# The order of the opening loads in a planned kernel: small parameters in front of the modulation weights and x rows

## The chip, the cores and the metric

The kernel runs on one core of one Trainium2 chip. The metric is the device time of one execution in microseconds; the time given is the median of three runs. Shorter is better.

## The reference

An x of 2048 tokens by 448 channels passes through two halves, each with an adaptive layer norm in front of it: a long convolution per channel, whose kernel is generated from state-space parameters, and a gated GELU block. Six modulation rows are computed from a small vector c.

```
x = A_u
mod = (_silu(c) @ w_mod).reshape(c.shape[0], 6, 1, -1)
sa, ca, ga, sb, cb, gb = (mod[:, 0], mod[:, 1], mod[:, 2], mod[:, 3], mod[:, 4], mod[:, 5])
h = _layernorm(x, axis=-1) * (1 + ca) + sa
x = x + ga * _A_ref(h, A_A_re, A_A_im, A_B_re, A_B_im, A_C_re, A_C_im, A_log_dt, A_Dskip)
h = _layernorm(x, axis=-1) * (1 + cb) + sb
x = x + gb * _B_ref(h, B_w_gate, B_w_up, B_w_down)
```

`_A_ref` makes, with dt = exp(log_dt), the convolution kernel K[d, l] as the real part of the sum over 256 states n of C dt B exp(dt A l), convolves it with h by an FFT of 4096 points, and adds h times Dskip. `_B_ref` is (gelu(h w_gate) * (h w_up)) w_down with an inner width of 1792.

## The kernel before, in words

The work is a list of 2018 small tasks, each a handful of instructions or DMAs on one engine. The function `s4_geglu` (line 413) makes them with `add` (line 473); each carries a name, an engine and its dependencies. Their order is written out by hand: the table `PLACE` (lines 40 to 263) gives every task a place, the n-th entry of a name for the n-th task of that name, and a letter behind the place picks the engine where there is a choice (a ACT, d DVE, p POOL, s SP). `Plan.order` (line 296) sorts by place and `Plan.run` (line 304) issues the tasks so. An engine works through its tasks in that order and waits at each for what it needs; tile buffers are also taken in that order.

The stages: an opening that loads parameters and rows; then, side by side, the generation of the convolution kernel (lines 629 to 755, 56 steps of exponentials, sines, products and small matmuls), the normalisation and first Fourier stage of x (lines 874 to 1006), and the transforms (lines 1068 to 1255); from about half of the span on the gated block (lines 1378 to 1680), bound by matmuls.

The tasks of the opening that matter here:

- p.ld.0 and p.ld.1 (`ld1`, lines 509 to 517, DMA at 512) load 448 and 224 KB of the state-space parameters for the first 112 channels, on ACT's queue. p.A1 (543) and p.A2 (548, 549) on DVE read the first; p.S1 (552, 553), p.S2 (570), p.S3 (571) on ACT, p.B1 (557 to 560), p.D1 (574 to 576) and p.B3 (579) on DVE follow; p.B2 (578) on ACT reads c.ld as well. dt (495, 496) on ACT reads c.ld, the log_dt vector. p.A3 (562) and p.C1 (565, 566) read p.ld.1 and dt. p.c0, d0, e0, f0 (481, 537, 539) split a result in three bfloat16 parts, which p.put0 (596) writes to DRAM from ACT's queue; lt0 (621) reads it back. p.put1 and lt1 do that with the second result.
- c.c (line 790) loads the vector c; silu (793) on ACT, which stands behind p.A3 in ACT's order, and sil2 (796 to 798) on DVE turn it into silu(c).
- m.ld.0, m.ld.1, m.ld.2 (`ldw`, line 806) load 784 KB of modulation weights each. m.mq0 (812) is the matmul of the third, m.cp0 (483) copies its partial sums, m.sm0 (823) adds them up; m.mm (816) makes the other two rows, with sixteen matmul instructions; m.ev (831, 834) evacuates, gs (860) multiplies two rows.
- x.ld.0 and x.ld.1 (853) load 896 KB of x each; bn (878, 879) takes their statistics, rstd (887) the roots, as (912) and norm (905) use them, ua (922) is the first Fourier matmul.
- c.ea (384 KB), c.rd (256 KB), c.au (64 KB), c.ak (128 KB; all through line 487) are constant tables; c.c and c.ld are 1.8 KB each. au is first read by as (912), ea and rd by the matmuls of lines 639 and 658, ak by line 771 much later.
- pad.0 (515) on POOL's queue copies 224 KB from DRAM to DRAM; d0 (865) and sel (842, 844) are memsets on POOL.
- p.ld.2 and p.ld.3 load 448 and 224 KB of parameters for the second 112 channels, from SP.

SP and ACT each own a queue for DMAs, and issue them in the order of their tasks. [...]

Of the kernel before, what the change touches and what calls it, by code (L numbers as in the profile page):

```python
# [40 lines left out]
    "anc": "121 137 143 162 152 204 207 247 264 309 333 340 348 356 445 456 469 485 502 517",  # L41
    "ang": "106 110 127 145 146 164 206 215 246 298 318 332 347 355 420 447 455 478 501 508 509 593 603 608 656 674 694 708 "
        "741 764 769 775 787 788 806 882 889 907 908 925 926 946 1005 1017 1018 1026 1039 1053 1114 1126 1135 1147 1153 1171 "
        "1184 1202",
    "as": "67d 75a 93d 109d 114d 130d 150a 176a 249d 254d 261a 283d 293d 329d 330d 352d",
    "bn": "45 46 59 57 39 47 48 55 230 236 232 234 184 228 196 201",
    "c.ai": "1266",
    "c.ak": "43",
    "c.au": "21",
    "c.c": "7",  # L50
    "c.ea": "20",
    "c.ih": "1280",
    "c.ld": "8",
    "c.rd": "25",
    "c.t1": "240",
    "co.adde": "1338 1339 1368 1340",
    "co.addl": "1383 1386 1419 1414",
    "co.addx": "1500 1510 1501 1520 1676 1714 1737 1684 1800 1812 1815 1806",
    "co.c2": "1586d 1593d 1587d 1590a 1758d 1760d 1772a 1770a 1893a 1907a 1906a 1900a",
    "co.ca": "1406a 1407a 1449a 1439a",  # L60
    "co.cb": "1415d 1413a 1452a 1441a",
    "co.h0": "1399a 1402a 1445d 1431a",
    "co.h2": "1534a 1576a 1568a 1557a 1750a 1746d 1761a 1766d 1855d 1888a 1842a 1874a",
    "co.l0": "1405 1411 1446 1432",
    "co.l2": "1538 1580 1570 1575 1752 1754 1762 1767 1856 1898 1851 1884",
    "co.mme": "1321 1335 1334 1337",
    "co.mml": "1378 1384 1408 1404",
    "co.mmx": "1488 1507 1489 1508 1653 1707 1735 1655 1791 1808 1810 1792",
    "co.n": "1390 1397 1444 1424",
    "co.nx": "1524 1573 1548 1532 1747 1745 1751 1763 1828 1876 1832 1872",  # L70
    "co.rc": "1389 1396 1427 1423",
    "co.rcx": "1522 1743 1825",
    "co.rt": "1387 1394 1421 1416",
    "co.rtx": "1521 1740 1816",
    "co.t2": "1560 1592 1571 1589 1755 1756 1765 1769 1882 1902 1868 1894",
    "co.ta": "1401 1403 1447 1437",
    "co.tb": "1409 1412 1448 1438",
    "cos": "523 609 624 635 686 687 713 711 756 773 798 797 805 820 819 887 902 910 924 940 950 957 1012 1028 1041 1044 1051 "
        "1066 1123 1133 1152 1167 1186 1195 1210 1225",
    "cos2": "126 141 144 163 158 205 213 256 276 317 334 342 354 359 446 463 482 488 506 530",  # L80
    "d.hi": "1564 1547 1584 1492 1528 1599 1502",
    "d.ld": "1562 1540 1582 1491 1514 1588 1497",
    "d.lo": "1569 1549 1585 1504 1533 1600 1513",
    "d0": "13",
    "dn": "1602 1605 1607 1608",
    "dn.k0": "1741 1889 1991",
    "dn.k2": "1753 1896 1998",
    "dn.k3": "1759 1899 2001",
    "dn.r": "1603 1606 1615 1631",
    "dn.r1": "1744 1962 2004",  # L90
    "dn.r4": "1768 1903 2002",
    "dn.r5": "1773 1908 2009",
    "dn.r6": "1775 1905",
    "dn.rh": "2003 2014 2016",
    "dn.s0": "2015",
    "dn.s1": "2017",
    "dn.st": "1650 1651 1621 1646 1774 1797 1786 1790 2008 2006 1979 1949 2011 2007 2010",
    "dn0": "1734 1738 1883 1886 1989 1990",
    "dn1": "1739 1891 1996",
    "dn2": "1764 1901 2005",  # L100
    "dn3": "1771 1904",
    "dn3h": "2012 2013",
    "dn4": "1749 1895 1999",
    "dn5": "1748 1892 1997",
    "dn6": "1757 1897 2000",
    "dsk": "195",
    "dt": "22",
    "e.f": "1664 1715 1702 1616 1645 1625 1683",
    "e.hi": "1666 1717 1703 1617 1652 1629 1687",
    "e.ld": "1649 1705 1700 1611 1644 1620 1679",  # L110
    "e.lo": "1667 1719 1704 1618 1658 1636 1689",
    "ev.end": "1252",
    "ev.fp": "705",
    "ev.geg": "1461",
    "ev.pq": "1332",
    "ev.ps": "1459",
    "ev.ub": "379",
    "ev.w0": "1369",
    "f.fc": "707 738 751 789 795 831 851 896 897 932 952 1019 1032 1060 1069 1105 1124 1142 1162 1180",
    "f.fwd": "740 757 780 809 834 850 877 898 917 945 964 995 1016 1033 1055 1076 1094 1118 1145 1154 1206 1214",  # L120
    "f.inv": "747 771 790 814 846 862 888 911 941 960 985 1013 1021 1050 1063 1089 1106 1129 1149 1173 1217 1232",
    "f.pr": "743 759 785 810 835 854 883 903 935 959 970 999 1020 1040 1062 1078 1104 1120 1148 1161 1207 1218",
    "f.st": "762 793 830 841 912 894 931 934 976 1008 1009 1030 1059 1090 1093 1112 1131 1157 1176 1190 1242 1241",
    "f.ut": "706 739 760 791 796 832 865 893 913 933 953 973 1006 1027 1035 1061 1079 1110 1130 1143 1174 1179",
    "f.z": "755a 774d 804a 822a 868a 866d 895d 922a 958d 982a 1000d 1014a 1038d 1052a 1084a 1098a 1125d 1140a 1164a 1188a "
        "1229a 1238a",
    "gs": "71 112",
    "gu": "1487 1498 1516 1517 1525 1542 1558 1559 1567 1578 1594 1614 1633 1634 1654 1656 1668 1671 1681 1685 1706 1710 "
        "1720 1721 1776 1777 1781 1793 1796 1809 1813 1823 1838 1839 1848 1853 1867 1869 1909 1912 1913 1922 1929 1931 1938 "
        "1939 1957 1958 1968 1969 1978 1980",  # L130
    "gu.g": "1429 1442 1450 1458 1463 1467 1474 1479 1496 1503 1518 1526 1543 1550 1563 1572 1583 1595 1609 1619 1635 1638 "
        "1657 1660 1672 1675 1686 1693 1708 1712 1722 1727 1778 1779 1784 1795 1804 1811 1822 1827 1841 1843 1857 1859 1875 "
        "1878 1910 1914 1918 1923 1930 1935 1943 1945 1959 1960 1970 1972 1981 1984",
    "gu.h0": "1475 1482 1515 1537 1555 1577 1597",
    "gu.ha": "1626 1642 1663 1680 1696 1716 1730 1783 1803 1817 1833 1847 1863 1880 1916 1934 1944 1948 1964 1975 1987",
    "gu.hs": "1628 1641 1665 1690 1698 1732 1733 1794 1818 1826 1846 1861 1870 1887 1921 1926 1952 1954 1982 1976 1994",
    "gu.l0": "1478 1485 1519 1539 1561 1579 1598",
    "gu.la": "1632 1643 1669 1682 1697 1726 1731 1788 1821 1830 1854 1852 1864 1881 1917 1941 1953 1956 1965 1983 1988",
    "gu.ls": "1630 1647 1673 1692 1701 1742 1736 1798 1819 1834 1850 1862 1873 1890 1927 1942 1967 1955 1993 1977 1995",
    "gu.m": "1430 1451 1454 1462 1464 1468 1476 1481 1506 1512 1523 1531 1545 1553 1565 1574 1591 1596 1610 1623 1637 1639 "  # L140
        "1659 1661 1674 1677 1691 1694 1709 1713 1723 1728 1780 1782 1789 1801 1805 1814 1824 1829 1844 1845 1858 1860 1877 "
        "1879 1911 1915 1919 1924 1936 1937 1946 1947 1961 1963 1971 1973 1985 1986",
    "gu.s": "1624 1640 1662 1678 1695 1718 1729 1785 1807 1820 1831 1849 1866 1885 1920 1925 1950 1951 1966 1974 1992",
    "gu2": "1422 1436 1443 1455 1456 1465 1466 1469",
    "ka": "217 275 302 364 374 407 462 516 572 606 717 720 745 792 836 884 915 949 951 990 1058 1072 1127 1172 1192 1216 "
        "1248 1249",
    "kd": "199 248 290 346 369 405 459 514 553 577 671 697 737 784 824 880 905 937 948 978 1047 1068 1115 1168 1183 1201 "
        "1244 1247",
    "kev": "185d 233d 282d 345d 368d 404d 431d 500a 548d 576d 665a 679d 735d 779a 818a 856a 890d 920a 947d 977d 1046d 1065a "
        "1107d 1144a 1182d 1196a 1224a 1246a",  # L150
    "kgen": "138 172 192 220 262 281 294 326 337 361 388 395 418 421 483 490 510 541 536 573 619 642 658 678 723 728 758 778 "
        "786 813 823 837 858 875 892 914 930 942 962 974 997 1025 1048 1057 1083 1099 1117 1136 1146 1163 1181 1194 1205 "
        "1213 1237 1240",
    "kout": "255a 285a 312a 376d 448a 410a 507a 525a 578d 632d 721d 734d 770a 808a 844a 891d 923a 956a 989a 994d 1075a 1109d "
        "1139a 1178a 1203a 1226a 1251d 1250a",
    "lt0": "60 165 324 366 568 763 870 972",
    "lt1": "82 194 336 402 701 842 975 1007",
    "m.cp": "531d 585a 812d",
    "m.cp0": "38d",
    "m.ev": "65 69 51 545 599 829",  # L160
    "m.ld": "6 19 11 419 549 750",
    "m.mm": "44 52",
    "m.mq": "528 583 772",
# [1668 lines left out]
```

## Time and profile before

| | before |
|---|---|
| three runs, us | 799.31, 800.68, 804.53 |
| the profiled execution, us | 800.69 |
| its span, first to last instruction, us | 798.7 |
| granted TensorE clock, mean | 0.995 |
| busy: TensorE, VectorE (DVE), ScalarE (ACT) | 92%, 74%, 58% |
| HBM read, written, MB | 100.39, 36.01 |

In the profile's rows, L with a number is the line of the kernel; PE is TensorE, PEld its weight loads, DVE VectorE, ACT ScalarE, POOL GpSimd, SP the engine that only issues DMAs. A row of the timeline has start and duration in us, engine, line, operation, output<-input, and in brackets the idle time before it and what ended it. SPq and ACTq are issues on these engines, not the transfers. A row of the chain of waits has start and duration of a piece of the chain that ended last; a DMA there lasts from its issue to its landing. A row of the waits has the engine and line that waited, what it waited for, and the total, number and longest of the waits in us. The row of the DMA queues has packets, MB and the time that they took as a share of sixteen engines; q1 is SP's queue, q10 ACT's, q0 POOL's.

### The profile page before, as it was taken

How to read it: one execution, taken by the hardware profiler on the slowest of the kernel's cores; microseconds unless marked ns; L12 is line 12 of the kernel's file. 1: busy time of each engine (PE TensorE's matmuls, PEld its weight loads, DVE VectorE, ACT ScalarE, POOL GpSimd, SP SyncE). 2: the span in 40 equal slices, each digit the busy share in tenths (PEclk: the TensorE clock that was granted, in tenths of full speed). 3: DMA queues.
4: the chain of work that ended last, by engine and by line, in shares of the span. 5: the costliest groups of instructions: out<-in, count | busy, mean ns of one | idle time of the engine just before them, and what ended most of it. 6: DMA issues, size and time to landing. Idle time of an engine off the chain costs nothing.

```text
span 798.7 us, 19205 instructions
## 1 busy us (share of the span) xinstructions
PE 731.0 (92%) x8262; PEld 448.9 (56%) x8262; DVE 594.1 (74%) x896; ACT 466.9 (58%) x620; POOL 9.1 (1%) x24
## 2 busy tenths in 40 slices
PE   0766789998899999989899999999999999999998
PEld 0333444444667777768774445444695446954478
DVE  3889999999999999989768851469773587133743
ACT  3699999899999999961655630233413243213320
POOL 0000000000000000001200000000000000000000
PEclk9999999999999999999999999999999999999999
DMA  9455458998887767998697663354407222012201
GB/s 265 126 163 154 129 138 252 266 285 237 233 259 225 210 196 220 288 295 243 200 303 238 231 170 129 127 165 153 156 12 220 92 93 93 2 47 92 82 1 59
DMA packets 91119, 136.74 MB, mean 171 GB/s; under 512 B 21716, under 2 KB 72596, under 8 KB 91034
## 3 DMA queue, kind: packets, MB, share of 16 engines
q1 hardware_dynamic: 85156, 127.32, 52.9%
q10 hardware_dynamic: 5318, 7.22, 2.8%
q8 instruction: 65, 1.06, 0.5%
q0 software_dynamic: 560, 0.98, 0.4%
q14 instruction: 20, 0.16, 0.1%
HBM read 100.39 MB, written 36.01 MB: 171 GB/s over the span
## 4 chain that ended last, share of the span: by engine, by line
PE 68%; ACT 10%; DVE 9%; DMA 8%; issue 3%; SPq 2%; ACTq 0%; DVEq 0%
PE pq L1528 30%; PE pq L1628 9%; PE pd L1597 4%; PE pf L1106 3%; PE kg L749 3%; DMA q<-in_abc 2%; DVE ty L726 2%; PE pg L676 2%; PE pf L1095 2%; PE pq L1522 2%; ACT fg L689 2%; DMA us<-uo 2%; PE kg L772 2%; PE pd L1628 2%; DMA ui<-u_d 1%
## 5 line engine op out<-in xcount | busy, mean ns | idle before, releaser
L1528 PE MATMUL pq<-ht,wr 128*128 128x512 f16 (+1 forms) x1200 | 248.6, 365 | 0.9 <-ACT ge L1535 0.9
L1528 PEld LDWEIGHTS <-wr 128*128 128x128 f16 x1200 | 114.5, 98 | 128.6 <-issue 11.9
L726 DVE TENSOR_TENSOR ty<-my,fg 128x2048 f32<-128x2048 f32 x56 | 127.5, 2282 | 0.9 <-ACT fg L700 0.3
L1542 DVE TENSOR_TENSOR fq<-ge,pq 128x512 f32<-128x512 f32 (+1 forms) x60 | 38.9, 649 | 72.7 <-PE pq L1528 45.6
L1535 ACT ACTIVATE ge<-pq 128x512 f32<-128x512 f32 (+1 forms) x60 | 34.0, 566 | 88.3 <-PE pq L1522 53.2
L1554 ACT ACTIVATE hh<-fq 128x1024 f16<-128x1024 f32 (+1 forms) x49 | 46.7, 961 | 62.1 <-DVE fq L1542 43.5
L1628 PE MATMUL pq<-d,hh 128*128 128x224 f16 x476 | 69.2, 259 | 0.0
L722 DVE TENSOR_TENSOR tx<-mx,fg 128x1024 f32<-128x1024 f32 x56 | 67.6, 1216 | 1.7 <-ACT fg L693 1.0
L749 PE MATMUL kg<-ty,tx 128*32 128x64 f32 x3584 | 62.9, 221 | 4.2 <-issue 2.4
L749 PEld LDWEIGHTS kg<-ty,tx 128*32 128x32 f32 x3584 | 53.4, 110 | 22.8 <-issue 14.4
L1557 DVE TENSOR_TENSOR hlo<-fq,hh 128x1024 f16<-128x1024 f32 (+1 forms) x49 | 53.7, 1105 | 15.4 <-ACT hh L1554 15.2
L1628 PE MATMUL pq<-d,hlo 128*128 128x224 f16 x238 | 61.6, 259 | 0.0
L689 ACT ACTIVATE fg<-pg 128x1024 f32<-128x1024 f32 x56 | 58.2, 1040 | 0.8 <-PE pg L676 0.4
L663 ACT ACTIVATE my<-pg 128x1024 f32<-128x1024 f32 x56 | 55.7, 1031 | 2.1 <-PE pg L658 1.9
L1628 PEld LDWEIGHTS <-hh 128*128 128x128 f16 x560 | 53.9, 98 | 0.6 <-issue 0.2
L1106 PE MATMUL pf<-q,fc 128*128 128x160 f32 x264 | 41.5, 307 | 1.1 <-DVE q L1099 1.1
L693 ACT ACTIVATE fg<-fg,small 128x1024 f32<-128x1024 f32 x36 | 41.6, 1173 | 0.1
L1106 PEld LDWEIGHTS pf<-q,fc 128*128 128x128 f32 x264 | 36.4, 190 | 6.6 <-issue 1.5
L676 PEld LDWEIGHTS <-lt 64*128 64x128 bf16 x304 | 17.9, 94 | 37.7 <-issue 25.3
L1745 ACT ACTIVATE d<-fq 128x896 f16<-128x896 f32 x14 | 13.2, 945 | 41.0 <-PE pd L1597 27.3
L676 PE MATMUL pg<-ea,lt 64*128 64x512 bf16 x152 | 30.5, 385 | 7.2 <-ACT fg L700 3.2
L985 PE MATMUL pf<-ui,fu 128*128 128x448 f32 x66 | 31.1, 575 | 1.7 <-ACT uo L481 1.4
(212 smaller groups left out, 1140.0 us busy)
## 6 DMA issues: line engine op xcount, KB each, us to landing
wr<-w_d SPq DMA_DIRECT2D x21, 896.0 KB
fc<-in_k_fc SPq DMA_DIRECT2D x20, 576.0 KB
u_d<-so SPq DMA_DIRECT2D x32, 224.0 KB
ui<-u_d SPq DMA_DIRECT2D x10, 672.0 KB
fq<-in_wd SPq DMA_DIRECT2D x14, 448.0 KB
w<-in_wgu SPq DMA_DIRECT2D x11, 512.0 KB
us<-uo SPq DMA_DIRECT2D x22, 240.0 KB
q<-us SPq DMA_DIRECT2D x22, 240.0 KB
```

The lines of the kernel that those rows point to most:

```text
L663: A.activation(yb.tile.rearrange("p h (n k) -> p n h k", n=2), pb.tile.rearrange("p (n h k) -> p n h k", n=2, h=2), AF.Exp)
L676: T.matmul(pa[:, nh * 512:nh * 512 + 512], w, x, start=(k == 0), stop=(k == 2))
L689: A.activation(fb.tile[:, 0].rearrange("p x (n k) -> p n x k", n=2), pb.tile.rearrange("p (n x k) -> p n x k", n=2, x=2), AF.Sin, scale=TW ...
L693: A.activation(fb.tile[:, 1], fb.tile[:, 1], AF.Sin, scale=-TWO_PI, bias=halfpi)
L722: V.tensor_mul(tx.tile, xb.tile[:, xm, None, :].to_broadcast([128, 2, 512]), fb.tile[:, :, 0])
L726: V.tensor_mul(ty.tile, yb.tile[:, :, None, :].to_broadcast([128, 2, 2, 512]), fb.tile[:, None, :, 1].to_broadcast([128, 2, 2, 512]))
L749: T.matmul(kg[32 * g:32 * g + 32, 2 * (s % 2) + q, :64], tx[:, r, nh, 4 * q + g], ty[:, 0:4:3, nh, 4 * q + g] if r else ty[:, 1:3, nh, 4 * ...
L1106: T.matmul(pz.tile[:, e % 32 - sl0], fc.tile[:, i, 1 + t], pp.tile[:, t, i], start=(t == 0 and e != 32), stop=(t == 1 and e != 0))
L1528: T.matmul(pb.tile[k][:, ts], wr.tile[:, 4 * lo + t, k, c0:c0 + 128], ht[:, m, ts], start=f % 2 == 0 and i == 0, stop=f % 2 == 1 and i == 9)
L1554: A.activation(hg.tile[0][:, cb, c], fq.tile[:, c], AF.Copy)
L1557: V.tensor_sub(hg.tile[1][:, cb, c], fq.tile[:, c], hg.tile[0][:, cb, c])
L1628: T.matmul(bank(k)[:, m], x[:, p, q[0], ts], w[:, p, q[1]], start=new and m == 0 and p == 0 and z == 0, skip_group_check=True, stop=i in ( ...
```

## The change

The operations stay as they are, on the same engines. All of `PLACE` is written anew, but sorted by engine the new places give the old order on PE and DVE throughout, and on SP, ACT and POOL everywhere but at the start:

| engine | before | after |
|---|---|---|
| SP | m.ld.0, c.c, c.ld, x.ld.1, m.ld.2, x.ld.0, m.ld.1, c.ea, c.au, c.rd, c.ak | c.c, c.au, c.ak, m.ld.0, c.ld, x.ld.1, m.ld.2, x.ld.0, m.ld.1, c.ea, c.rd |
| ACT | p.ld.0, p.S1, p.ld.1, p.S2 | p.ld.0, p.ld.1, p.S1, p.S2 |
| POOL | d0, pad.0, sel | pad.0, d0, sel |

Across engines the new places also swap five pairs of neighbours in the order in which tile buffers of one kind are taken: m.ld.3 and ang.14, m.ld.5 and mag.8 (tile fg), f.z.4 and f.z.5 (zo), two ua.ev (so), two t.z0 (z0). In the opening the buffer of p.ld.1 is taken ahead of that of p.A1. The entries of the diff that carry this:

```
-    "c.ak": "43",
-    "c.au": "21",
-    "c.c": "7",
+    "c.ak": "5",
+    "c.au": "4",
+    "c.c": "2",
...
-    "c.ld": "8",
-    "c.rd": "25",
+    "c.ld": "7",
+    "c.rd": "22",
...
-    "m.ld": "6 19 11 419 549 750",
...
-    "p.S1": "4 101 323 550",
...
-    "p.ld": "0 15 80 81 171 315 491 499",
...
-    "pad": "14 237 313 794",
...
+    "m.ld": "6 19 12 423 539 727",
...
+    "p.S1": "16 105 328 547",
...
+    "p.ld": "0 9 65 86 140 291 490 507",
...
+    "pad": "10 203 278 785",
...
-    "x.ld": "12 9 208 166",
...
+    "x.ld": "18 8 201 139",
```

414 rows, old and new, of the table PLACE are left out of this document.

## The prediction

> **What bounds the kernel now.** I read the page first, then the chain of waits over the first 70 us, then SP's issues, the two compute engines of the opening, and last the DMA queues in short windows.
>
> ```profile
> span 798.7 us, 19205 instructions
> ...
> DMA  9455458998887767998697663354407222012201
> ...
> PE 68%; ACT 10%; DVE 9%; DMA 8%; issue 3%; SPq 2%; ACTq 0%; DVEq 0%
> ```
>
> The 800.69 us execution has a span of 798.7 us, so 1.99 us lie outside it; the median of the runs shown is 800.68, the same. The chain is TensorE for two thirds, but that is a mean over stages. The change touches the first 25 us, where the first slice of the DMA row is full (9). There the chain of waits reads:
>
> ```profile
> 0.75 7.87 DMA q<-in_abc
> ...
> 10.70 9.71 DMA q<-in_abc
> ...
> 20.44 0.02 ACT q L562
> ...
> 20.85 0.19 ACT sig L793
> 21.04 0.57 ACT lh L481
> ...
> 23.72 0.55 DVE zo L483
> ...
> 24.40 1.83 PE pf L823 x2
> 26.23 7.83 PE pf L816 x16
> ...
> 34.09 0.55 ACT gs L834
> 34.66 0.64 DVE gs L860
> ```
>
> Two parameter loads, p.ld.0 (448 KB) and p.ld.1 (224 KB), hold the chain for 7.87 and 9.71 us. The second, the smaller one, takes longer: it is issued at 10.70, behind S1 in ACT's order, when SP has already queued the modulation weights and rows. At 20.44 it lets A3 go (L562). Behind A3 in ACT's order stands silu (L793), so the modulation matmuls wait for it too, though they don't read it. From 26.2 to 34.1 TensorE computes two modulation rows (L816), and then the first normalisation can start. The engines had been ready long before:
>
> ```profile
> 16.49 0.20 ACT L496 ACTIVATE dts__106<-dts__106 112x4 f32<-112x4 f32 x1
> ...
> 18.44 0.42 DVE L579 TENSOR_TENSOR q<-q 112x256 f32<-112x256 f32 x1
> ...
> 21.49 0.16 DVE L798 TENSOR_TENSOR c_sb<-c_sb,sig 112x4 f32<-112x4 f32 x1
> ```
>
> ACT has finished dt at 16.69 and DVE has finished B3 at 18.86; both then idle to 20.4 and later. How the DMA engines were shared, in windows 2.0 to 7.7, 10.7 to 15.5 and 15.5 to 19.3 us (packets, MB, share of the 16 engines):
>
> ```profile
> q1 hardware_dynamic: 299, 0.86, 50.7%
> q10 hardware_dynamic: 127, 0.46, 31.6%
> ...
> q1 hardware_dynamic: 213, 1.37, 100.6%
> ...
> q1 hardware_dynamic: 132, 0.79, 78.2%
> q10 hardware_dynamic: 127, 0.23, 24.6%
> ```
>
> And the rate, in the last column, of the first 2 us and of 8 to 22 us (ahead of it PEclk and the DMA share):
>
> ```profile
> 0.00:2.00 2.00, 0.00 (x0) 0.00 (x0) 0.09 (x2) 0.00 (x0) 1.13 (x7) 1.00 0.22 29
> ...
> 8.00:22.00 14.00, 0.29 (x4) 0.20 (x8) 6.90 (x15) 7.99 (x14) 0.00 (x0) 1.00 1.03 297
> ```
>
> q1 is SP's queue, q10 ACT's. p.ld.0 needs 31.6% of 5.7 us, that is 1.8 us of all sixteen engines, but is stretched over 5.7 us beside SP's 0.86 MB; it lands at 8.62, 0.9 us after the window that holds its packets. Next to nothing moves in the first 2 us, so an issue at 0.75 has its first packets 1.25 later. p.ld.1 moves nothing at all for the first 4.8 us after its issue (SP's queue alone fills the engines), and then needs 24.6% of 3.8 us, or 0.93 us. The opening as a whole moves a fixed number of bytes at some 297 GB/s; so a new order can't shorten the whole, it decides only who waits.
>
> **The change, part by part.** Nothing is added or removed. Four things move: c.c, c.au and c.ak to the front of SP; p.ld.1 ahead of S1 on ACT, right behind p.ld.0; c.ld behind the first w_mod load; and on POOL pad ahead of d0's memset. SP's rows of before:
>
> ```profile
> 1.22 0.41 SPq L487 DMA_DIRECT2D c_sb<-in_c  x1
> ...
> 8.63 0.31 SPq L806 DMA_DIRECT2D fg<-in_w_mod  x1
> ...
> 11.74 0.33 SPq L487 DMA_DIRECT2D rd<-in_k_rd  x1
> 14.90 0.33 SPq L487 DMA_DIRECT2D ak<-in_k_ak  x1
> ```
>
> ```profile
> SPq L806 <- DMA q<-in_abc: 4.4, 1, 4.4
> SPq L487 <- DMA fg<-in_w_mod: 2.8, 1, 2.8
> ```
>
> *p.ld.0.* Beside it now stand c.c, c.au and c.ak, 194 KB in place of 0.86 MB. Its start at 2.0, its own 1.8 and the 0.9 of landing give 4.7 with no sharing; the small loads add at most 194 KB at 297 GB/s, 0.65. I take 5.5. The bounds are 4.7 and today's 8.6.
>
> *p.ld.1* follows in the same queue: 0.93 later, 6.5, and with the rest of the small loads 7. It is needed when dt is done, so it leaves the chain.
>
> *The chain after it.* What ran from 8.64 to B3's end at 18.86 hangs on p.ld.0 and moves by 8.6 - 5.5 = 3.1, to 15.75. c.ld has to be there for B2 (15.86 - 3.1 = 12.8); behind 784 KB of w_mod it lands at about 10, and is covered by 2.8 us. A3 and silu follow dt at 13.6 and are done by 14.2. Then c0 starts at 15.8 in place of 20.98 (5.2 earlier), and sil2, three short operations from 21.07 to 21.65, ends at 16.35.
>
> *The first modulation matmul* (m.mq0) also needs its weights, m.ld.2. It landed by 14.90, where ak's issue was let go. Ahead of it now stand p.ld.1 (0.93) and c.au with c.ak (192 KB, 0.65): 16.5. Its issue, the ninth on the two queues, waits for the first load as m.ld.1's does today (8.63), so until 5.5: no hole. Bounds: 14.9, and 17.7 if each of the three issues put ahead (0.41) is lost as well. I take 16.6; so the matmul starts at 16.7 and not 21.71, **5.0 us earlier**, and the weights are now what is late next, by 0.3 us.
>
> *From there* order and engines are as before, so what hangs on it moves by 5.0, if no other load is late:
>
> ```profile
> 23.75 0.32 ACTq L596 DMA_DIRECT2D lh_d<-lh  x1
> ...
> 26.02 0.62 DVE L878 BATCH_NORM_STATS2 st<-xt 128x6 f32<-128x448 f32 x1
> ...
> 29.47 1.36 ACTq L621 DMA_DIRECT2D lt<-lh_d  x2
> 30.85 1.28 ACT L887 ACT_TABLE_LOAD   x1 [0.84 <-issue]
> 32.59 0.30 ACT L887 ACTIVATE rs<-mv,small 128x8 f32<-128x8 f32 x1 [0.45 <-DVE mv L879]
> ...
> 33.28 0.29 DVE L912 TENSOR_SCALAR as<-au,rs 128x128 f32<-128x128 f32 x1
> ```
>
> x.ld.0 (896 KB, 3.1 us behind m.ld.2) lands at 19.7 and is read at 26.02 - 5.0 = 21.0. m.ld.1 (784 KB, 2.7) lands at 22.4, at 23.5 if p.put0's packets (336 KB) come between; it is read by the second half of the sixteen matmuls, from about 25. c.ea and c.rd, 640 KB more, land at 25 to 26 and are read at 29. DVE's own work ends with L912 at 28.6, so TensorE still sets the end of the stage. What is least covered is p.put0: ACT issues it at 23.75 - 5.0 = 18.7, while SP's queue is still full, and lt0 waits for its landing, at 29.47 - 5.0 = 24.5 on ACT. I put the landing at 24.5 to 25.5: 1.25 from issue to first packet, 3.5 to 4.5 one for one with SP's packets (p.ld.1 took 3.8), then 0.9. Behind lt0 on ACT stand the table load, rs and the evacuations of L834; lt0's 1.36, the load's 1.28, 0.30 for rs and 0.55 for the first evacuation end at 33.0 if nothing else waits, 1.1 us before the chain needs ACT at 34.09. So a landing up to 25.6 is covered. That c.c, c.au, c.ak and pad come earlier brings nothing: their readers wait for others (silu for ACT's order, L912 for rs).
>
> *The sum.* 5.0 us less at L860, minus 0.1 for p.put0: 4.9. Nothing later hangs on absolute time: every engine keeps its order, so the rest moves with it. Five pairs of neighbours later on change the order in which they take tile buffers, m.ld.3 (L806) with ang.14 the first:
>
> ```profile
> 118.83 2.28 DVE L726 TENSOR_TENSOR ty<-my,fg 128x2048 f32<-128x2048 f32 x1
> ...
> 124.90 0.48 SPq L806 DMA_DIRECT2D fg<-in_w_mod  x1
> ```
>
> The buffer that m.ld.3 now gets is the one that this product was the last to read; it is free 3.8 us before m.ld.3's issue. I price the five at nothing, within 1 us either way. Span 798.7 - 4.9 = 793.8; with the 1.99 outside **795.8 us**, 0.6% less, where about 1% is what a measurement of this kernel can tell from no change.
>
> **A rule on the clock.** TensorE's sixteen matmuls don't run at one speed (weight loads, start and duration):
>
> ```profile
> 29.01 0.34 PEld L816 LDWEIGHTS pf<-fg,c_sb 112*128 112x128 f32 x1 [0.41 <-issue]
> 29.75 0.19 PEld L816 LDWEIGHTS pf<-fg,c_sb 112*128 112x128 f32 x1 [0.40 <-issue]
> 30.13 0.19 PEld L816 LDWEIGHTS pf<-fg,c_sb 112*128 112x128 f32 x1 [0.18 <-issue]
> ```
>
> They come every 0.75 us up to 29.0 and every 0.375 behind. All slow they would take 12 us, all fast 6; they take 8.0. I let that pattern move along. [...]
>
> **The rivals.** *First, the small loads cost more than their bytes*, and the weights behind them set the chain. For it: each load pays 1.25 us to start and 0.9 to land. If three paid these 2.15 in a row, m.ld.2 would land at 14.9 + 0.93 + 6.45 = 22.3, 0.6 behind today's start of the matmul: 801.3; with half of it 2.5 behind the forecast, 798.3. Against it: c.c's issue takes 0.41 and the engines stay full. [...] No run so far shows such a load alone.
>
> *Second, slower: ACT stands at lt0.* p.put0 is queued behind everything of SP. Today p.ld.1 in that position took 9.71 us for 224 KB; taken by size, 336 KB would take 14.6, from 18.7 to 33.3. ACT is in order, so lt0, rs, the row of L834 and all exponentials would then be late by what exceeds 29.47 and the 1.1 of slack, 2.7 us behind today: 803.4. It is slower as soon as the landing passes 30.6. Against it: at 10.70 the loads issued ahead came to 5.4 MB, of which 2.5 had moved (8.7 us at up to 297 GB/s), 2.9 left; at 18.7 all of the opening and p.ld.2 behind it come to 6.5 MB, of which 5.0 have moved, 1.5 left.
>
> *Third, the clock.* All sixteen slow adds 4.0 us to the forecast (799.8), all fast takes 2.0 off (793.8).
>
> *Fourth, the gain is absorbed later*, or p.ld.1 is still served last and the order on paper doesn't reach the engines: 800.7. Against it: SP's and ACT's issues of before stand in the trace as written.
>
> **How the numbers follow.** The forecast (a gain of 4 to 6) gets 0.57, the first rival 0.15, the second 0.06, the third 0.14, halved between its two ends, the fourth 0.08. The low end is the clock's best (793.8), p.ld.0 without sharing (0.8 less) and 1.5 us for scatter (the three runs lie between 799.31 and 804.53): 791.5. The high end is the first rival in full, 801.3. Over 1% faster (below 792.7) needs all the luck at once: 0.08. Over 1% slower (above 808.7) needs more than the second rival: 0.04. The rest, 0.88, lies within 1%.
>
> **What would show it.** Right: A1 (L543) starts near 5.5, A3 at 13.6, L812 near 16.7, L860 near 29.7, the first load of 53.33 (L621) near 48.4, and the end 4.9 earlier. L812 late with c_sb ready means the first rival; lt0 waiting on p.put0 the second; L816's sixteen longer or shorter than 8.0 the third; a move of 5 at L860 that is gone by 200 us the fourth. A move under 1 us at A1 would refute the sharing that I read from the windows.

## The result, and the profile after

The changed kernel takes 796.84 us (median of 13 runs, 794.71 to 800.76) beside 800.68 for the kernel before (13 runs, 798.3 to 804.53): a ratio of 0.995, with a 95% interval of 0.9935 to 0.9966. That is a gain of 0.5%, under the 1% that the prediction took for what a measurement can tell; with thirteen runs on each side the interval still leaves out no change. The execution that was profiled took 795.67 us; its span is 793.8, with the granted clock at 0.995 as before.

The page of the changed kernel gives its span and the shares of its chain:

```profile
span 793.8 us, 19204 instructions
...
PE 64%; DVE 6%; ACT 5%; DMA 3%; issue 3%; SPq 0%; DVEq 0%; ACTq 0%
```

This chain can be followed back only to 147.7 us, and its shares add up to 81%, so they can't be held against those of before, and it says nothing of the opening. This is the timeline of the changed kernel there (start, duration, engine, line, operation; in brackets the idle time and what ended it):

```profile
5.35 1.23 DVE L543 TENSOR_TENSOR q<-q 112x1024 f32<-112x1024 f32 x1 [4.43 <-DMA q<-in_abc]
...
13.31 0.49 ACT L562 ACTIVATE q<-q,dts__106 112x256 f32<-112x256 f32 x1
...
16.12 1.72 PE L812 MATMUL pf<-fg,c_sb 112*32 112x448 f32 x8 [16.12 <-DVE c_sb L798]
...
18.44 0.32 ACTq L596 DMA_DIRECT2D lh_d<-lh  x1
...
20.72 8.31 PE L816 MATMUL pf<-fg,c_sb 112*128 112x448 f32 x16
...
25.68 1.37 ACTq L621 DMA_DIRECT2D lt<-lh_d  x2
...
27.08 1.28 ACT L887 ACT_TABLE_LOAD   x1 [2.37 <-issue]
...
29.07 0.54 ACT L834 ACTIVATE gs<-pf 128x448 f32<-128x448 f32 x1
29.64 0.62 DVE L860 TENSOR_TENSOR gs<-gs,rows 128x448 f32<-128x448 f32 x1 [0.41 <-ACT gs L834]
...
47.68 2.08 SPq L621 DMA_DIRECT2D lt<-lh_d  x2
```

A1 (L543) starts at 5.35 and not 8.64. A3 (L562) no longer waits for p.ld.1: it follows dt at 13.31, 7.1 us earlier than its 20.44. The first modulation matmul (L812) starts at 16.12 in place of 21.71. L860, where the stage ends, comes at 29.64 in place of 34.66, and the first load of lt0.1 (L621) at 47.68 in place of 53.33, where 48.4 was forecast.

Behind that the two executions run in parallel. The same three instructions on DVE, before and then after:

```profile
199.58 1.29 DVE L539 TENSOR_TENSOR lh<-q,lh 112x512 bf16<-112x512 f32 x2
...
369.83 0.69 DVE L1201 TENSOR_TENSOR my<-my,pf 64x512 f32<-64x512 f32 x1
...
424.72 0.18 DVE L1419 BATCH_NORM_AGGREGATE mv<-st 128x2 f32<-128x6 f32 x1
```

```profile
194.58 1.28 DVE L539 TENSOR_TENSOR lh<-q,lh 112x512 bf16<-112x512 f32 x2
...
364.48 0.69 DVE L1201 TENSOR_TENSOR my<-my,pf 64x512 f32<-64x512 f32 x1
...
419.91 0.18 DVE L1419 BATCH_NORM_AGGREGATE mv<-st 128x2 f32<-128x6 f32 x1
```

The differences are 5.00, 5.35 and 4.81 us; the gain at L860 was 5.02. What was won in the first 30 us is still there 170 us later to 0.02 us. After that it swings by about a microsecond: 5.35 here, 6.1 on DVE's instructions between 390 and 411 us, and 4.8 from 425 us to the end. The last long piece of TensorE in the chain of waits, before and after:

```profile
774.81 16.10 PE pq L1628 x168
```

```profile
770.01 16.10 PE pq L1628 x168
```

It starts 4.80 us earlier and takes the same time.

### The profile page after: what moved, and what is told of

The parts are those of the page before. It is cut to its first block, busy times and chain, and to the rows that moved or that the text cites. A ratio compares the mean times of both kernels' runs of the same rounds, so it can differ in the third digit from the quotient of the medians.

```text
span 793.8 us, 19204 instructions
## 1 busy us (share of the span) xinstructions
PE 731.5 (92%) x8262; PEld 449.3 (57%) x8262; DVE 594.2 (75%) x896; ACT 466.6 (59%) x620; POOL 9.0 (1%) x24
## 4 chain that ended last, share of the span: by engine, by line
PE 64%; DVE 6%; ACT 5%; DMA 3%; issue 3%; SPq 0%; DVEq 0%; ACTq 0%
PE pq L1528 28%; PE pq L1628 9%; PE pd L1597 4%; PE pf L1106 3%; PE kg L749 3%; PE pf L1095 2%; PE kg L772 2%; PE pg L676 2%; PE pq L1522 2%; DMA yi<-y 2%; DVE ty L726 2%; PE pd L1628 2%; PE pd L1405 1%; DVE tx L722 1%; DVE q L1099 1%
## 5 line engine op out<-in xcount | busy, mean ns | idle before, releaser
L1106 PE MATMUL pf<-q,fc 128*128 128x160 f32 x264 | 41.5, 307 | 1.2 <-DVE q L1099 1.2
```

Of the source, the lines that this page charges most:

```text
L1106: T.matmul(pz.tile[:, e % 32 - sl0], fc.tile[:, i, 1 + t], pp.tile[:, t, i], start=(t == 0 and e != 32), stop=(t == 1 and e != 0))
```

## The experiments

Twelve more kernels were run, one of them the changed kernel again, each beside the kernel before on the same chip. In most of them every place of the table is multiplied by ten and a table MOVE gives some tasks another one. That shifts all lines by one: L544 there is L543 here, L813 is L812, L817 is L816, L861 is L860 (in e5, e9 and e11 the later lines shift by a few more).

```
+MOVE = {("p.ld", 1): 25}
...
-        self.at, e = int(at.rstrip("adps")), at[-1]
+        self.at, e = MOVE.get((n, i), 10 * int(at.rstrip("adps"))), at[-1]
```

| run | median, us | ratio to before, 95% interval | A1 | A3 | m.mq0 | sixteen: start, length | lt0 | L860 |
|---|---|---|---|---|---|---|---|---|
| before | 800.68 | | 8.64 | 20.44 | 21.71 | 26.02, 8.03 | 29.47 | 34.66 |
| after | 796.84 | 0.995 (0.9935–0.9966) | 5.35 | 13.31 | 16.12 | 20.72, 8.31 | 25.68 | 29.64 |
| after again | 798.66 | 0.9962 (0.9942–0.9983) | 5.45 | 13.41 | 16.22 | 20.82, 7.20 | 25.22 | 29.12 |
| e1 p.ld.1 alone | 800.41 | 0.9972 (0.995–0.9993) | 8.59 | 16.56 | 19.36 | 23.96, 6.85 | 27.40 | 32.10 |
| e2 small loads alone | 799.84 | 0.9972 (0.995–0.9994) | 5.24 | 19.29 | 21.03 | 25.20, 7.12 | 31.38 | 35.27 |
| e3 opening only | 798.67 | 0.995 (0.9927–0.9973) | 5.75 | 13.72 | 16.52 | 21.12, 7.74 | 25.55 | 29.47 |
| e4 c.au, c.ak back | 798.07 | 0.9941 (0.992–0.9963) | 5.83 | 13.79 | 16.60 | 21.20, 8.52 | 26.38 | 30.34 |
| e5 w_mod in quarters | 798.37 | 0.9947 (0.993–0.9964) | 6.07 | 14.03 | 16.84 | 21.43, 8.20 | 25.63 | 30.24 |
| e6 silu early | 799.83 | 0.9969 (0.9949–0.999) | 5.51 | 13.48 | 16.87 | 21.04, 7.95 | 26.30 | 30.19 |
| e7 full reorder | 801.86 | 0.9998 (0.998–1.0017) | 5.71 | 14.67 | late row | 13.71, 7.89 | 26.26 | 29.73 |
| e8 put0 on SP | 798.11 | 0.9942 (0.9921–0.9963) | 5.40 | 13.37 | 16.64 | 20.82, 8.48 | 24.26 | 29.91 |
| e9 x.ld.0, m.ld.1 in quarters | 800.74 (one run) | | 5.24 | 13.21 | 16.83 | 21.00, 7.31 | 25.46 | 29.34 |
| e10 put0 first | 800.19 | 0.9974 (0.9954–0.9994) | 5.59 | 13.56 | 13.68 | 17.85, 4.75 and 5.92 | 21.08 | 32.40 |
| e11 warm-up | 811.43 | 1.0122 (1.0094–1.015) | 5.32 | 13.29 | 23.45 | 26.07, 6.18 | 30.31 | 35.01 |

The medians of before beside these runs were 801.97 to 803.38, so only ratios compare across rows; intervals that overlap, which most do, separate nothing. The spans that the expectations name are reckoned from the 798.7 us of the first profile and can't be held against these runs for the same reason. The theories are told apart by the start times of the opening.

**One part at a time (e1, e2, e3).** e1 is the kernel before with p.ld.1 moved ahead of S1 and nothing else (the diff above). e2 has only the small loads in front, and e3 both, with pad, and all later places as before:

```
+MOVE = {("c.c", 0): 52, ("c.au", 0): 53, ("c.ak", 0): 54}
...
+MOVE = {("p.ld", 1): 25, ("c.c", 0): 52, ("c.au", 0): 53, ("c.ak", 0): 54, ("pad", 0): 125}
```

> Theory (two parts: the small loads shield p.ld.0, and p.ld.1's place frees A3): with p.ld.1 alone moved ahead of S1, p.ld.0 still shares with w_mod and lands near 8.6; p.ld.1 is there by 12, dt is done at 16.7 and B3 at 18.9, so c0 starts at 18.9 in place of 20.98: 2.1 us earlier at L860 and at the end, span 796.6. Rival (p.ld.1's place on ACT is the whole effect): 4.9 us, span 793.8.

> Theory: with c.c, c.au and c.ak in front and p.ld.1 still behind S1, p.ld.0 lands near 5.4 and p.ld.1 is issued at 7.4, but behind SP's backlog; it lands at 14 to 17.5 where dt is done at 13.4, so A3 waits for it again and the gain is 3.5 to 5, span 794 to 795. Rival (p.ld.1's place is all): no gain, span 798.7.

> The table of before with nothing but the opening's moves on SP, ACT and POOL; the five later swaps of tile buffers are undone. Theory: the same as the whole change, span 793.8 within 0.5. Rival (the later swaps carry part of it, or cost something): over 1 us away from 793.8.

The timeline of e1, of the kernel with w_mod still first:

```profile
8.59 1.23 DVE L544 TENSOR_TENSOR q<-q 112x1024 f32<-112x1024 f32 x1 [7.68 <-DMA q<-in_abc]
```

And of e2:

```profile
5.24 1.23 DVE L544 TENSOR_TENSOR q<-q 112x1024 f32<-112x1024 f32 x1 [4.33 <-DMA q<-in_abc]
7.30 0.33 ACTq L513 DMA_DIRECT2D q<-in_abc  x1
19.29 0.51 ACT L563 ACTIVATE q<-q,dts__106 112x256 f32<-112x256 f32 x1 [6.00 <-DMA q<-in_abc]
```

e1 frees A3 and wins 2.6 us at L860 (34.66 to 32.10), though A1 stays at 8.59. e2 wins 3.4 us at A1 and little behind it: p.ld.1 is now issued at 7.30, 3.4 us earlier than before, and yet A3 waits for it until 19.29, 1.2 us earlier than before. The sixteen matmuls end at 32.32, 1.7 earlier. L860 is even 0.6 later than before, and that has another cause: p.put0, issued at 22.61, has its first packet at 26.0, and ACT stands at lt0 for about 2 us, with rs and L834's rows behind it:

```profile
31.38 1.37 ACTq L622 DMA_DIRECT2D lt<-lh_d  x2
```

Together (e3) the two parts win 5.2 at L860. They are not terms of a sum: most of what the early A1 brings is lost again while p.ld.1 stands behind it. e3, with before's later places, gives the same opening and the same ratio as the whole change, so the five swapped pairs of neighbours are worth nothing that shows. At the end the parts are not told apart: e2's median lies 0.3% under that of before, as far as e1's, in spite of its opening. Its profiled execution, at 804.23 us, was its slowest, and why its median gains is open.

**What lets p.ld.0 through (e4, e5).** e4 takes c.au and c.ak, 192 of the 194 KB, back to their old places behind c.ea and c.rd in the changed kernel:

```
+MOVE = {("c.au", 0): 205, ("c.ak", 0): 225}
```

> The changed kernel with c.au and c.ak back behind c.ea and c.rd, c.c alone in front. Theory (the 192 KB of small loads are what keeps w_mod off p.ld.0): p.ld.0 lands near 8 again, c0 starts near 18.3, gain 2.1 to 2.7, span 796 to 796.6. Rival (the small loads are only in the way, 0.65 us of bytes and their fixed costs): gain 5 to 6, span 793 or less.

A1 starts at 5.83, 0.5 later than in the changed kernel, but 2.8 earlier than in e1. So 1.8 KB of c.c in front do most of what the prediction ascribed to having 194 KB in place of 0.86 MB beside p.ld.0. The DMA queues show why. In the kernel before, from 3 to 4 us (packets, MB, share of the 16 engines):

```profile
q1 hardware_dynamic: 28, 0.20, 50.6%
q10 hardware_dynamic: 28, 0.11, 42.7%
```

In the changed kernel from 2 to 3 us, and then from 3 to 4:

```profile
q10 hardware_dynamic: 37, 0.15, 52.2%
q1 hardware_dynamic: 57, 0.00, 2.6%
...
q10 hardware_dynamic: 90, 0.30, 88.2%
q1 hardware_dynamic: 80, 0.03, 16.0%
```

Before, the two queues moved one packet for one: 28 and 28. w_mod's packets are 7 KB (0.20 MB over 28) and p.ld.0's 4 KB (0.11 over 28), so SP got nearly two thirds of the bytes though ACT had as many packets. After, SP's queue is busy with the packets of c.c, of c.au and c.ak, 57 that move next to nothing and 80 that move 0.03 MB, and ACT's queue gets 88% of the engines from 3 to 4 us. With c.c alone in front (e4), SP's queue moves 82 packets from 2 to 3 us, at 3.9% of the engines and with 0.00 MB, and ACT's moves 0.14 MB; in e1 they move 0.07 and 0.06 MB there. So the 1.8 KB cost SP's queue most of that microsecond, and the time went to the transfer that matters. Whether it costs by the packet or by the load is not told apart by these three loads.

If the packets count, small ones must do it without any small load. e5 is e1 (w_mod first at 0.75, p.ld.1 early) with the first w_mod load cut into four:

```
-            dma(wb.tile, a["w_mod"][i])
+            for t in range(4) if i == 2 else ():
+                dma(wb.tile[:, t], a["w_mod"][i][:, t])
+            if i != 2:
+                dma(wb.tile, a["w_mod"][i])
```

> The kernel with p.ld.1 alone moved, where w_mod stands first and nothing is in front of it, but the first w_mod load cut into four DMAs whose packets are 1.8 KB and not 7 KB; p.ld.0's stay at 4 KB. If the two queues take turns packet by packet, p.ld.0's 448 KB pass with about 200 KB of w_mod beside them, and L543 starts at 5 to 6, as with the small loads in front, instead of 8.59. If they share by bytes, or if the queue that issues first is served first, w_mod's first 784 KB still stand beside p.ld.0 and L543 stays at 8 to 8.6. The time follows the first modulation matmul: near 799 in the first case if the weights (m.ld.2) don't come later, near 800.5 in the second.

A1 starts at 6.07 and not 8.59, with nothing in front of w_mod. The queues from 2 to 5 us in e5:

```profile
q10 hardware_dynamic: 140, 0.49, 52.1%
q1 hardware_dynamic: 182, 0.30, 37.3%
```

0.49 MB of ACT's queue have passed, more than p.ld.0's 448 KB, beside 0.30 MB of w_mod; in e1 the same three microseconds have 0.26 and 0.48. That the bytes in front decide, or the queue that issues first, or the 0.47 us by which c.c delays w_mod's issue, is refuted by it; that each of the four pieces costs SP's queue a fixed time is not. L860 comes at 30.24, and the time, a ratio of 0.9947, can't be told from that of the whole change.

The counts agree with a share that goes by packets more than by bytes; strictly one for one it isn't (37 to 57 above). 28 and 28 in one microsecond are fewer than two from each queue on each of the 16 engines; the trace doesn't tell the engines apart, so how one engine goes between the two queues is not shown.

**What was late next (e6).** silu and sil2 go to the front of ACT and DVE in the changed kernel:

```
+MOVE = {("silu", 0): 95, ("sil2", 0): 105}
```

> The changed kernel with silu in front of p.S1 on ACT and sil2 in front of p.A1 on DVE, so that c_sb is ready near 5. It asks what was late next behind silu. If the weights are (as the prediction had it), m.mq0 (L812) starts at m.ld.2's landing; by the changed kernel's records that is near 15.9, 0.2 earlier than 16.12, and nothing later gains more than 0.2. If the weights had much time in hand, L812 starts well before 15. The end moves by 0 to 0.3 against the changed kernel, because p.put0's landing (lt0 at 25.7) holds ACT in front of L834 as before.

The timeline of e6:

```profile
16.87 1.72 PE L813 MATMUL pf<-fg,c_sb 112*32 112x448 f32 x8 [16.87 <-DMA fg<-in_w_mod]
```

With c_sb ready at 4.85, the matmul starts at 16.87, when the weights land, and not near 15.9. So they had no time in hand: they are what the matmul waits for at 16.87 here, 16.64 in e8 and 16.83 in e9. In the changed kernel they were there by 16.12, when c_sb came; the two are late nearly together. Behind that e6 falls back further, from 0.55 us behind the changed kernel at L861 to 1.97 at the load of L622 at 61.15 (L621 at 59.18 there). This has another cause. In windows 33 to 37 us (busy time of PE, PEld, DVE, ACT and POOL, then PEclk, DMA share, GB/s), the changed kernel and then e6:

```profile
33.00:37.00 4.00, 2.29 (x16) 1.05 (x15) 3.96 (x8) 4.00 (x6) 0.00 (x0) 1.00 0.45 99
```

```profile
33.00:37.00 4.00, 4.00 (x17) 2.21 (x15) 2.69 (x5) 3.18 (x5) 0.00 (x0) 0.50 0.24 56
```

TensorE was granted half its clock there (in e6 from 31.4 to 45.1 us), and for a stretch it was the bound in place of DVE and ACT: DVE's busy time falls from 3.96 to 2.69.

**The write that lt0 waits for (e8, e9).** In the changed kernel the DMA queues in windows 21 to 22, 22 to 23 and 23 to 24 us:

```profile
q1 hardware_dynamic: 168, 0.37, 98.6%
...
q1 hardware_dynamic: 93, 0.29, 108.0%
q10 hardware_dynamic: 2, 0.01, 2.2%
...
q10 hardware_dynamic: 64, 0.19, 58.3%
q1 hardware_dynamic: 37, 0.12, 39.9%
```

p.put0 is issued at 18.44 and has its first two packets just before 23, some 4.5 us later; then it has the larger part of the engines and is through within two more. p.ld.1 did the same before (issue 10.70, nothing to 15.5), and so it did in e2 (issue 7.30, nothing to 12). In the kernel before, where SP's queue moved only 0.10 MB from 23.75 to 24.6, at 41.5% of the engines, p.put0 was issued at 23.75 and had its first packet 0.8 us later; from 24 to 25 us there:

```profile
q10 hardware_dynamic: 38, 0.12, 40.6%
```

In e1 it took 1.7 us (21.68 to 23.34), with some 0.7 MB of SP's left, an estimate reckoned as in the prediction (6.5 MB, less 297 GB/s since 2.0 us). e8 issues p.put0 from SP, ahead of c.ea and c.rd:

```
+MOVE = {("c.ea", 0): 382, ("c.rd", 0): 384}
...
-                (adma if t == 0 else dma)(lh_d[t, e, :, :6], lb.tile)
-            return add("p.put%d" % e, {"ACT" if t == 0 else "SP": 0.42}, v0 + dv * k, go, dep, use=[lb], kb=344)
+                (adma if t == 0 and e else dma)(lh_d[t, e, :, :6], lb.tile)
+            return add("p.put%d" % e, {"ACT" if t == 0 and e else "SP": 0.42}, v0 + dv * k, go, dep, use=[lb], kb=344)
```

> The changed kernel with p.put0 issued by SP instead of ACT, in SP's order behind m.ld.1 and ahead of c.ea and c.rd. In the changed kernel p.put0 is issued on ACT's queue at 18.44 and moves nothing until 22.9, while SP's queue works off 1.3 MB that were issued before it. If it is this backlog that holds it, p.put0 now has only m.ld.1 in front of it: it lands near 22.7 to 23.5 in place of 25.6, lt0 (L622) goes at 24.7 to 25.0 without a wait of its own, right behind p.c1, the table load of L888 ends near 27.3, and L861 is held by the sixteen matmuls of L817 alone, at 29.0 to 29.4 where these take 8.3. c.ea and c.rd land 1.5 us later than before, near 25, and don't hold L640. The end: 0.3 to 1 us less than the changed kernel (796 to 797). If a write from ACT's queue is slow by itself, or the write is slow wherever it is queued, lt0 stays near 25.7 and nothing is gained.

The timeline of e8:

```profile
16.64 1.72 PE L813 MATMUL pf<-fg,c_sb 112*32 112x448 f32 x8 [16.64 <-DMA fg<-in_w_mod]
...
20.82 8.48 PE L817 MATMUL pf<-fg,c_sb 112*128 112x448 f32 x16
...
24.26 1.36 ACTq L622 DMA_DIRECT2D lt<-lh_d  x2
...
29.34 0.54 ACT L835 ACTIVATE gs<-pf 128x448 f32<-128x448 f32 x1 [1.22 <-PE pf L817]
```

lt0 goes at 24.26, as soon as ACT comes to it, 1.4 us earlier than in the changed kernel, so the write is not slow by itself; together with the 0.8 and 1.7 us above this shows that what held it was SP's backlog on the other queue. L861 wins nothing from it (29.91), for the sixteen matmuls are then the only thing late: ACT waits 1.22 us for them.

e9 asks whether the hold is a number of packets or of bytes: x.ld.0 and m.ld.1 cut into quarters, in the changed kernel, as w_mod was in e5:

> The changed kernel with x.ld.0 and m.ld.1, the two big loads that SP has queued when p.put0 is issued, cut into four DMAs each: the same bytes in packets of 1.8 KB and not 7 KB. If the 4.4 us in which p.put0 moves nothing are a fixed number of packets accepted before it, they shrink to less than half and p.put0 lands before 24, lt0 is let go at 24.7 by ACT's own order. If they are bytes issued before it, the first packets still come near 22.9 and lt0 stays at 25.2 to 25.9.

From 21 to 22 us ACT's queue moves 20 packets, so the hold is near 3 us in place of 4.5; lt0 still goes at 25.46. That lies between the two expectations. The cut loads also made SP late, so that c.rd was issued behind p.put0 (18.88 and 18.34). What the hold is made of stays open.

**Orders built on this (e7, e10).** Both were meant to beat the change; their start is that silu goes first, B3, d0 and f0 ahead of D1, and DVE's row statistics into its gaps. e7 loads x.ld.1 first and the third modulation row last; e10 puts p.put0 on SP ahead of m.ld.1. The orders on SP:

```
changed: c.c c.au c.ak m.ld.0 c.ld x.ld.1 m.ld.2 x.ld.0 m.ld.1 c.ea c.rd p.ld.2
e7:      c.c c.au c.ak x.ld.1 m.ld.0 c.ld m.ld.1 x.ld.0 c.ea c.rd p.ld.2 m.ld.2
e10:     c.c c.au c.ak m.ld.0 c.ld m.ld.2 x.ld.1 x.ld.0 p.put0 m.ld.1 c.ea c.rd p.ld.2
```

> An opening ordered by what the runs showed so far: silu and sil2 first; x.ld.1 ahead of the w_mod loads; the two rows that the first normalisation needs (m.mm.0, m.mm.1) ahead of the third, whose load goes last; B3, d0 and f0 ahead of D1 on DVE; the row statistics in DVE's gaps. By the rows of the changed kernel p.put0 is issued near 16.5 in place of 18.44, lands near 22 to 23 in place of 25.6, and L860 starts near 25 in place of 29.64. If the end still hangs rigidly on the opening, 793 to 794; if DVE and ACT, busy 97% from 46 us on, take the gain back, 796 to 797; if the third row, now late, holds the second normalisation (L861, 39.54), 798 or more.

> An opening that uses both findings: silu first, m.ld.2 ahead of the rows of x (so that L813 starts near 13), B3, d0 and f0 ahead of D1 so that p.put0 can go near 16.5, and p.put0 on SP ahead of m.ld.1, c.ea and c.rd, which are issued behind it. By backlog p.put0 lands near 20 and lt0's data near 24; the sixteen matmuls start near 17.5 and end near 25.5; L861 near 26.5 to 27.5 in place of 29.6, if DVE's row statistics are done by 27. If the rest then moves as one piece, the end comes 2 us earlier than in the changed kernel, 794 to 795.5. If TensorE falls back to half speed between 30 and 38, as in the two reordered versions before (L923 1.86 us for four matmuls in place of 1.02), the gain is gone again: 797 or more.

In e7 the sixteen matmuls end at 21.6, and nothing comes of it: p.put0, issued at 17.97, is held again, lt0 goes at 26.26, the roots for the normalisation stand behind it on ACT, and L861 comes at 29.73. Of the 4.9 us by which L861 is ahead of the kernel before, 2.5 are gone by 52 us, and at the end nothing is left; the clock was at half from 23.9 to 34.1 us, and what else costs e7 its lead is open. In e10 lt0 goes at 21.08, but SP had stood at p.put0's place in its order until 18.08 and let the queue run dry. The queue of e10 from 16.5 to 18 us, and its second eight matmuls:

```profile
q1 hardware_dynamic: 24, 0.09, 14.3%
```

```profile
25.87 5.92 PE L817 MATMUL pf<-fg,c_sb 112*128 112x448 f32 x8 [3.27 <-DMA fg<-in_w_mod]
```

m.ld.1 is then what is late, and L861 falls to 32.40. Neither is ahead of the changed kernel: each brings one chain forward and pushes another of the four that meet at L860 and L905 (weights, write and read back, statistics, matmuls) behind it.

**The clock (the changed kernel again, e11).** The changed kernel was run a second time as it is:

> The changed kernel once more, beside the others on one chip: median near 797, a ratio of 0.995 against before, L543 near 5.4, L812 near 16.1, L860 near 29.6. It measures how far two runs of the same order differ in the sixteen matmuls of L816 (8.0 before, 8.3 after) and in the stage from 340 to 430 us, where the other versions had a lower granted clock (0.91 in 340 to 360).

The sixteen matmuls took 7.20 us there and 8.31 in the first profile, in the same order on the same data: their weight loads pass from 0.75 to 0.375 us apart at 23.0 in one and at 25.1 in the other. The profile's clock column doesn't show this first half-speed stretch; it reads 1.00 there from the start. e11 adds to e8 work that nobody reads, 24 matmuls of au by au, in front of the first modulation matmul:

```
+    wu = Buf("pf")
+
+    def warm_up():
+        wu.tile = fft.tile([128, D], FT, name="pf")
+        for _ in range(24):
+            T.matmul(wu.tile[:, :384].rearrange("p (a b) -> p a b", b=128), au, au[:, None].to_broadcast([128, 3, 128]),
+                     start=True, stop=True)
+    add("wu", {"PE": 8.0}, -5.7, warm_up, [c_au], [wu])
```

> The version with p.put0 on SP, and in front of L813 24 more matmuls of au by au (128x384, results read by nobody), so that TensorE is busy from au's landing near 5.6 to about 15 instead of idle to 16. It takes away what is now late at L861, the sixteen matmuls of L817 at mixed speed (8.48 us there, 8.31 and 7.20 in two runs of the changed kernel). If the granted speed rises after some microseconds of uninterrupted work, as the switch in the midst of the sixteen suggests, the warm-up itself speeds up near its fifth or sixth matmul, L813 takes about 0.9 us in place of 1.72, L824 0.9 in place of 1.83, the sixteen near 6.0, and L861 comes at 28.3 to 28.6 in place of 29.91, then held by DVE's last statistics (L888 at 27.4). The end comes 1 to 1.5 us before that of the version with p.put0 on SP, near 796.5 beside 798.1. If the switch does not depend on the work in front of it, the sixteen stay at 7.2 to 8.5 and L861 at 29 to 30; if the 24 run at half speed throughout they last 16 us and L813 is late, at 21 or more: 802.

The timeline of e11:

```profile
5.88 17.64 PE L881 MATMUL pf<-au 128*128 128x384 f32 x48 [5.88 <-DMA au<-in_k_au]
...
23.45 0.96 PE L814 MATMUL pf<-fg,c_sb 112*32 112x448 f32 x8
...
25.24 0.99 PE L825 MATMUL pf<-zo,small 128*128 128x448 f32 x2 [0.84 <-DVE zo L485]
...
26.07 6.18 PE L818 MATMUL pf<-fg,c_sb 112*128 112x448 f32 x16
```

As an improvement it failed: each of the 24 became two instructions, which was not reckoned with, and they held TensorE to 23.5. The clock can be read from it all the same. The weight loads of the warm-up come every 0.64 us up to 9.24 and every 0.32 from 9.81 on, 3.9 us after its start; from there L814 takes 0.96 us in place of 1.72, L825 0.99 in place of 1.83, and the sixteen 6.18, one every 0.375 throughout. The 811.43 us are not the price of the late start alone (L862 comes at 35.01, 0.35 later than in the kernel before): 5.7 us more go in one hole near 132 us, where TensorE stands at L751 for 4.3 us without a cause that the profile shows, and which isn't in e8. That hole stays open, so nothing is read from the end of this run. What sets the switch is not shown: it came 3.4 to 3.9 us into the warm-up here, and between the two runs of the changed kernel, whose sixteen start at 20.82 and 20.72, it moved by 2.1 us.

## Why the prediction was right, step by step

*p.ld.0 lands at 5.5.* It did (A1 at 5.35), for a reason that was half wrong: the step "194 KB in place of 0.86 MB" counts bytes. The runs showed in its place that the queues share by packets more than by bytes (e4, e5). By bytes, e4 would have been back near 8.6; it was at 5.83, and e5, with the same bytes in smaller packets, at 6.07 where e1 has 8.59.

*p.ld.1 leaves the chain.* Right: A3 at 13.31 beside a forecast of 13.6, and c0 at 15.67 beside 15.8. e2 shows that without this move A3 still waits until 19.29, e1 that it alone is worth half at L860.

*The first modulation matmul at 16.7, held by the weights.* It started at 16.12, with m.ld.2 issued at 5.34, when p.ld.0 had landed (5.5 in the forecast), and the release was booked to c_sb; e6 and e8 then had it held by the weights at 16.87 and 16.64. So in the changed kernel's own profile the bound was c_sb and not the weights, which were there by then; that the two meet within a few tenths was right, and which of them is last changes from run to run.

*From there as before, 8.0 us for the sixteen.* 8.31 in the profile, 7.20 in the second. The third rival came, but not in its size: without a warm-up the sixteen lay between 6.85 and 8.52 in all versions that ran them in one piece on weights already there, so it is worth about a microsecond at L860 and not four or two. In no profile were all sixteen slow, and all fast only behind the warm-up of e11, at 6.18; what sets the switch no run shows.

*p.put0 lands at 24.5 to 25.5, and up to 25.6 is covered.* lt0 went at 25.68, ACT having stood there for about a microsecond, and L834's second row started at 29.07, where the last of the sixteen ended at 29.03. Slack and landing were right to a tenth, again with a wrong picture: not side by side with SP's packets from the start, but nothing for 4.5 us and then fast. That the two come to the same landing is luck. This is the mildest form of the second rival; in e2, where ACT stood at lt0 until 31.38, it came in earnest. Its price by size (14.6 us) was far off, for the hold hung on SP's backlog and not on the size: 4.9 us for 224 KB, 4.5, 1.7 and 0.8 for 336 KB.

*The first rival, small loads that cost more than their bytes.* Its premise holds: SP's queue moved next to nothing from 2 to 3 us (57 packets at 2.6% of the engines). Its conclusion doesn't, because the time went to p.ld.0, and nothing on the chain stood behind SP's queue by more than a few tenths.

*c.ld, c.ea, c.rd covered; the swaps and pad nothing.* None of them shows up as a wait in the changed kernel's opening; e3 leaves the swaps out and has the same gain.

*The rest moves rigidly.* 5.00 us at 195 us, 4.80 at the end, with a swing to 6.1 in between; the sum said 4.9, and a span of 793.8 is what was measured. The fourth rival, a gain absorbed later, didn't come in this profile. Other profiles lose part of their lead on the first profile of before: the second run of the changed kernel was 6.25 us ahead up to 335 us and 5.0 at the end, and e3 fell from 5.1 to 1.6 between 340 and 425. That doesn't show the gain absorbed, for the medians of before beside them are 1.3 to 2.7 us longer than in the first session, and e3 keeps a ratio of 0.995 to it. One cause shows. In the window 340 to 360 us, the changed kernel and then e3:

```profile
340.00:360.00 20.00, 17.26 (x332) 15.32 (x332) 15.83 (x23) 7.63 (x11) 0.00 (x0) 1.00 0.90 291
```

```profile
340.00:360.00 20.00, 16.48 (x304) 14.41 (x303) 13.62 (x17) 8.25 (x12) 0.00 (x0) 0.91 0.82 276
```

The granted clock is 0.91 for e3 there (0.91 to 0.93 for e1, e4, e8, e9 and e11 too) and 1.00 for the first two profiles. The 0.91 is a mean. In narrower windows of e3 it is 1.00 and then 0.50:

```profile
341.70:345.11 3.41, 1.33 (x58) 1.08 (x47) 3.10 (x3) 1.04 (x2) 0.00 (x0) 1.00 0.59 178
345.11:348.52 3.41, 3.41 (x24) 2.55 (x22) 2.10 (x3) 1.15 (x2) 0.00 (x0) 0.50 0.87 312
```

So TensorE ran at half clock for 3.41 us, behind 3.41 us in which it was busy for only 1.33. That costs up to 1.7 of the 2.8 us that e3 loses up to 360 us. The second run of the changed kernel has such a stretch at 337 to 340 us, and e5, e7, e8 and e9 have one near 470 us; in e8:

```profile
469.19:472.60 3.41, 3.41 (x9) 1.18 (x8) 2.29 (x3) 1.90 (x2) 0.00 (x0) 0.50 1.03 305
```

These four each lose 1.7 us between 450 and 500 us, where all the others lose nothing.

The median came out 1.0 us above the forecast, 796.84 and not 795.8, while the profiled execution hit it (795.67), which is luck in part. What the other executions lost is not shown, since only one of each is traced; stretches of half clock, 1.7 us each, are a candidate.

## What to carry to other kernels

When two queues share the DMA engines, count packets as well as bytes: here the queue with 7 KB packets took two thirds of the bytes beside one with 4 KB (0.20 and 0.11 MB, 28 packets each), and cutting the big transfer or putting small loads of many packets in front of it let the critical one land 2.5 to 3.4 us earlier (e5 against e1, e2 against before). A transfer that was issued on ACT's queue while SP's had 1.3 to 1.4 MB to move first moved nothing for 4.5 to 4.8 us (p.put0 after, p.ld.1 before); so issue early what the chain needs, as p.ld.1 here, rather than make its issue cheaper or its work faster. And look for the operations that stand behind a waiting instruction only by the engine's order: silu, which needs neither load, came 7.1 us earlier with A3. What moving silu alone would have brought in the kernel before was not tried.

## What the runs showed of the hardware that was not expected

- In three stretches two queues had nearly equal numbers of packets, though not of bytes: 78 and 77 from 3 to 6 us before (0.56 and 0.32 MB), 132 and 127 from 15.5 to 19.3 (0.79 and 0.23 MB), and in e2, from 14 to 16 us with p.ld.1 on ACT's queue:

```profile
q1 hardware_dynamic: 58, 0.36, 77.9%
q10 hardware_dynamic: 58, 0.12, 27.6%
```

- p.put0 after, and p.ld.1 before and in e2, had no packet for 4.5 to 4.9 us from their issue, in which SP's queue moved 1.31 MB at 102% of the engines (after, 18.44 to 22.9) and 1.37 MB at 100.6% (before, 10.7 to 15.5); p.put0 in the kernel before had its first after 0.8 us, in which SP's queue moved 0.10 MB (23.75 to 24.6).
- The weight loads of e11's warm-up passed from 0.64 to 0.32 us apart 3.4 to 3.9 us after its start. TensorE was at half clock from 31.4 to 45.1 us in e6, where the changed kernel was so only from 42.1 to 45.5.
- A granted clock of 0.91 over 20 us in e3 was a stretch of 3.41 us at half clock. The kernel before has two such stretches in its middle, from 46.80 and 203.81 us, and the changed kernel two, from 42.07 and 199.09, each of 3.41 us; in the 3.41 us ahead of them TensorE was busy for 1.42, 1.42, 1.42 and 1.61 us (1.33 in e3). In e6 and e7 the half clock lasted 13.7 and 10.2 us (31.4 to 45.1, 23.9 to 34.1). Whether the same stage of the kernel meets this changes from one execution to the next: from 340 to 360 us the clock was 1.00 in the first two profiles and 0.91 in e1 and e3. Near 470 us, where TensorE was busy throughout (3.41 of 3.41 us in e8), it cost 1.7 us in each of four runs.
